# A decode layer's last product in two column groups instead of four, its last weights and a slice of wq cut over other numbers of DMA engines

## The chip, the core and the metric

The kernel runs on one core of one Trainium2 chip. The metric is the device time of one execution in microseconds (us). The core has a matrix engine (PE, with its weight loads PEld), a vector engine (DVE), an activation engine (ACT), a general engine (POOL) and a sequencer that here only issues transfers (SP). Transfers run on 16 DMA engines that all queues share. A transfer that SP issues goes into a queue; each DMA engine that takes part works off its rows in the order of issue and then counts a semaphore up by one.

## What is computed

One decode step (8 batches, one token each) of a layer: attention over the last 2,048 keys of a cache with 32 query heads and 8 key heads, then a feed-forward block. All inputs are bf16. Cut to what is computed:

```python
def A(x, k_cache, v_cache, wq, wo):                  # x: 8 x 1 x 512
    W = 2048
    q = (x @ wq).reshape(8, 1, 32, 128)              # wq: 512 x 4096
    k, v = k_cache[:, :, -W:], v_cache[:, :, -W:]    # 8 x 8 x 2048 x 128 each, heads repeated 4 times
    p = softmax(einsum("bhqd,bhkd->bhqk", q, k) * 128 ** -0.5)
    return einsum("bhqk,bhkd->bhqd", p, v).reshape(8, 1, 4096) @ wo

def B(x, w1, w2, w3, w4):
    # the shifted branch (w1, w2) is zero for one token: x1 = x
    return x + gelu(layernorm(x) @ w3) @ w4          # w3: 512 x 1792, w4: 1792 x 512

h = A_x + A(layernorm(A_x), k_cache, v_cache, wq, wo)
out = h + B(layernorm(h), w1, w2, w3, w4)
```

## The kernel before

The program for each engine is a list written out in the order in which the Python runs; an operation waits for the semaphore values that it names (`Engine.op`, L57, `emit`, L63). There is no scheduler.

**Transfers.** All but x are issued by SP, in one fixed order (L767 to L776): wq, three K tiles, then V and K tiles in turn, three pieces of wo among the last V tiles, w3, and three pieces of w4. A K or V tile is 2 MB, 128 rows of 16 KB; there are 16 of each, in three buffers each, so that a load waits until PE has read what lay in its buffer before. Where nothing else is said a load has 128 rows.

**wq** lies with four of its 512 rows on each of 128 partitions. `load_wq` (L750) brings it in one load without the last `QF` = 1,152 columns of each partition's fourth row; six small loads (the table `FILL`, L44) bring these columns of the 128 rows into `wqF` (L143), a view of the space that w3 will have later. In an entry `(k, h, n)` the source list has `k` outer entries of four rows each, `h` says which 32 partitions and `n` which of `NF` = 3 sections. POOL clears sections 1 and 2 first (L216), and loads with `n` > 0 wait for that.

**Query.** x is normalized and turned (`xlnT`, L263). For the fill the matching columns of x are copied out (`xlnP`, L281), turned by PE (L286) and copied into `xlnF` (L291). PE multiplies wq (L301) in four column groups of 32 output rows that run side by side, then the fill rows (L312) into the second of the two result banks. The result is scaled (L322 ACT, L325 DVE), turned (L335) and laid out (L341, L349).

**Attention.** For each K tile PE turns the keys (L382), ACT and DVE bring them to SBUF (L392, L394), PE makes the scores (L407); softmax runs on DVE and ACT; PE multiplies with V (L503). PE, ACT and DVE do this while the transfers go on.

**End.** After the last V tile come the product with wo (L552), the layer norm (L638 to L682), the product with w3 (L667), gelu (L692, L694) and the product with w4. The residual is added by PE: the sum so far, in two bf16 parts (`fr`, L702 and L703), is multiplied by the identity into the same PSUM space (`pe_fin`, L707). w4 has 14 chunks of 128 rows and comes in pieces of 8, 4 and 2 chunks (`W4_AT`, L715, `load_w4`, L761); the product waits for one semaphore per piece. A chunk is four matmuls of 128 columns, each in a column group of its own (32 PSUM partitions). `pe_fin` stands between the first and the second piece. Then the four results are copied to `out_sb` (L729 to L734), two by DVE and two by ACT, and SP stores them (L779). `warm_end` (L489) puts matmuls without a use between steps; they write to a bank that nobody reads then.

Of the kernel before, what the change touches and what calls it, by code (L numbers as in the profile page):

```python
# [6 lines left out]
dt = mybir.dt  # L7
ACT = mybir.ActivationFunctionType
# [3 lines left out]
B = 8  # L12
D = 512
H = 32
DH = 128
# [7 lines left out]
FC = F // 128  # L23
FG = FC // 2
KC = D // 128
# [14 lines left out]
QW = H - 2 * NQ * R + 1  # L40
QE = QW + NQ * R + NQ * R + QW
AHEAD = NS
QF = 1152
FILL = ((8, 0, 0), (8, 1, 0), (8, 0, 1), (3, 1, 1), (3, 0, 2), (2, 1, 2))  # L44
NF = 3
KF = 64


# [30 lines left out]
def bass_sequential_preLN__sliding_block_cached__mixer_s_mlp__decode_kernel(  # L79
# [23 lines left out]
    with es:  # L103
        sb = lambda shape, dtype, name: es.enter_context(nc.sbuf_tensor(name, shape, dtype))
# [6 lines left out]
        ident_b = sb([128, 128], dt.bfloat16, "ident_b")  # L111
# [9 lines left out]
        w4_sb = sb([128, FC, D], dt.bfloat16, "w4_sb")  # L121
# [17 lines left out]
        rstd = sb([B, 1], dt.float32, "rstd")  # L139

        xlnF = sb([KF, NF, 32], dt.bfloat16, "xlnF")
        xlnP = sb([B, 4 * sum(k for k, _, _ in FILL)], dt.bfloat16, "xlnP")
        wqF = w3_sb[0:KF, 2:4, :].rearrange("p a n -> p (a n)")[:, 0:NF * QF].rearrange("p (s n) -> p s n", s=NF)  # L143
        xlnT = sb([128, KC, 32], dt.bfloat16, "xlnT")
        qrow = sb([128, 2, 512], dt.bfloat16, "qrow")
# [37 lines left out]
        fr = qflat[:, 0:2 * KC * 32].rearrange("p (a n x) -> p a n x", a=2, n=KC)  # L183
        gT = qflat[:, 2 * KC * 32:(2 * KC + FC) * 32].rearrange("p (f x) -> p f x", f=FC)
        out_sb = orow[0:B, 0, :]
# [12 lines left out]
        sem_wf = S("sem_wf")  # L198
# [5 lines left out]
        def dma(eng, dst, src, sem, *waits):  # L204
            def f(e):
                e.dma_start(dst, src).then_inc(sem, 16)  # L206
            eng.op(f, *waits, inc=False)
# [5 lines left out]
        PO.op(lambda e: e.memset(eps2[:], EPS * EPS))  # L213
        e_scr = PO.op(lambda e: e.memset(scratch[:], 1.0))
        e_fz = PO.op(lambda e: e.memset(xlnF[:], 0.0))
        e_wz = PO.op(lambda e: e.memset(wqF[:, 1:NF, :], 0.0))  # L216
        e_xz = PO.op(lambda e: e.memset(xlnT[:], 0.0))
        e_iota = PO.op(lambda e: e.iota(iota_f[:], [[1, 128]], base=0, channel_multiplier=-1,
                                        allow_small_or_imprecise_dtypes=True))
# [50 lines left out]

        def fills():
            at = 0
            for k, h, n in FILL:
                yield k, slice(32 * h, 32 * h + 4 * k), n, at, slice(at, at + 4 * k)
                at += 4 * k

        def q_rows():
            for k, rows, n, at, where in fills():
                a = xln_b[:, :]
                cols = bass.AP(tensor=a.tensor, offset=a.offset + KC * at + KC - 1, ap=[a.ap[0], [KC, k], [KC * k, 4]])  # L280
                e_xP = DV.op(lambda e, cols=cols, where=where: e.tensor_copy(  # L281
                    xlnP[:, where].rearrange("b (e a) -> b e a", a=4), cols))

            def pe_fT(e):
                for k, rows, n, at, where in fills():
                    ins = e.matmul(fT_ps[rows, n * B:(n + 1) * B], xlnP[:, where], ident_b[0:B, 0:B],  # L286
                                   is_transpose=True, tile_position=(0, rows.start))
                return ins
            e = PE.op(pe_fT, e_xP)
            for k, rows, n, at, where in fills():  # L290
                e_fT = DV.op(lambda e, rows=rows, n=n: e.tensor_copy(xlnF[rows, n, 0:B], fT_ps[rows, n * B:(n + 1) * B]),  # L291
                             e, e_fz)
            out = []
            for j in range(2):
                def pe_q(e, j=j):
                    for kc in range(KC):
                        for u in range(4):
                            n = (4 * j + u) * R * DH
                            size = R * DH if kc < KC - 1 else max(0, min(R * DH, H * DH - QF - n))
                            if size:  # L300
                                ins = e.matmul(S_ps[j][32 * u:32 * (u + 1), 0:size], xlnT[:, kc, :], wq_v[:, kc, n:n + size],  # L301
                                               start=(kc == 0), stop=(kc == KC - 1 and size == R * DH),
                                               tile_position=(0, 32 * u), skip_group_check=True)
                    return ins

                def pe_qF(e):
                    for n in range(NF):
                        for u in range(4):
                            w = (u - 4) * R * DH + QF
                            lo = max(0, -w)  # L310
                            if lo < R * DH:
                                ins = e.matmul(S_ps[1][32 * u:32 * (u + 1), lo:R * DH], xlnF[:, n, :],  # L312
                                               wqF[:, n, w + lo:w + R * DH], start=False, stop=(n == NF - 1),
                                               tile_position=(0, 32 * u), skip_group_check=True)
                    return ins
                e_q = PE.op(pe_q, e_xT, (sem_wq, 16))
                if j == 1:
                    e_q = PE.op(pe_qF, e_fT, (sem_wf, 16 * len(FILL)))
                got = S_ps[j][:, :].rearrange("p (r d) -> p r d", r=R)
                for c in range(2):  # L320
                    if j == 0:
                        e = AC.op(lambda e, c=c, got=got: e.activation(qrow2[:, 0, :, c, :], got, ACT.Copy, scale=inv_sqrt_dh),  # L322
                                  e_q)
                    else:
                        e = DV.op(lambda e, c=c, got=got: e.tensor_scalar(qrow2[:, 1, :, c, :], got, inv_sqrt_dh, None,  # L325
                                                                          ALU.mult), e_q)
                out.append(e)
            return out, e_q
# [160 lines left out]
        def warm_end(count):  # L489
            def f(e):  # L490
                for n in range(count):
                    ins = e.matmul(kbank[1], ident_b[:, :], still, start=True, stop=True)  # L492
                return ins
            PE.op(f, e_pT[LAST, 1])
# [178 lines left out]
                      free[2])  # L673
        warm_end(3)
        e_y = [pe_w3(0, FH, e_u, (sem_w3, 16)), pe_w3(FH, FC)]
        warm_end(4)

        e_vs = DV.op(lambda e: e.tensor_reduce(vsum[:, :], vr(st2), AX.X, ALU.add), e_st2)

# [9 lines left out]
        e_gT = []  # L689
# [12 lines left out]
        e_fr = DV.op(lambda e: e.tensor_copy(fr[:, 0, :, 0:B], v3(fin[:, :])), e_fin, e_gz)  # L702
        e_fr = DV.op(lambda e: e.tensor_tensor(fr[:, 1, :, 0:B], v3(fin[:, :]), fr[:, 0, :, 0:B], ALU.subtract), e_fr)  # L703

        z_ps = S_ps[1][:, 0:DH]

        def pe_fin():  # L707
            def f(e):
                for part in range(2):
                    for nb in range(KC):  # L710
                        ins = e.matmul(z_ps[32 * nb:32 * (nb + 1), :], fr[:, part, nb, :], ident_b[:, :],
                                       start=False, stop=False, tile_position=(0, 32 * nb), skip_group_check=True)
                return ins
            PE.op(f, e_fr)
        W4_AT = (0, 8, 12, FC)  # L715
        for n, waits in enumerate(((*e_gT, free[1]), (), ())):
            lo, hi = W4_AT[n:n + 2]
            def pe_w4(e, lo=lo, hi=hi):
                for fc in range(lo, hi):
                    for nb in range(KC):  # L720
                        ins = e.matmul(z_ps[32 * nb:32 * (nb + 1), :], gT[:, fc, :],
                                       w4_sb[:, fc, nb * 128:(nb + 1) * 128], start=(fc == 0), stop=(fc == FC - 1),
                                       tile_position=(0, 32 * nb), skip_group_check=True)
                return ins
            if n == 1:
                pe_fin()
                warm_end(1)
            e_z = PE.op(pe_w4, (sem_w4[n], 16), *waits)
        for nb in range(KC):  # L729
            to, got = out_sb[:, nb * 128:(nb + 1) * 128], z_ps[32 * nb:32 * nb + B, :]  # L730
            if nb % 2:
                e_outa = AC.op(lambda e, to=to, got=got: e.activation(to, got, ACT.Copy), e_z)
            else:
                e_outd = DV.op(lambda e, to=to, got=got: e.tensor_copy(to, got), e_z)  # L734

        def load_k(j):
            dma(SP, knat[:, j % NK, :],
# [12 lines left out]
        def load_wq():  # L750
            size = KC * H * DH - QF
            dma(SP, wbig[:, 0:size], A_wq.rearrange("(p k) n -> p (k n)", k=KC)[:, 0:size], sem_wq)
            for k, rows, n, at, where in fills():
                dma(SP, wqF[rows, n, :],
                    bass.AP(tensor=A_wq.tensor, offset=A_wq.offset + (KC * at + KC - 1) * H * DH + H * DH - QF,
                            ap=[[KC * H * DH, k], [KC * k * H * DH, 4], [1, QF]]), sem_wf, e_wz if n else None)

        def load_w3():
            dma(SP, w3_sb[:, :, :], B_w3.rearrange("(k p) f -> p k f", p=128), sem_w3, e_qturn)
# [1 line left out]
        def load_w4(n):  # L761
            lo, hi = W4_AT[n:n + 2]
            k = W4_RUN[-1] if hi == FC else W4_RUN[0]
            dma(SP, w4_sb[:, lo:hi, :].rearrange("p (g k) n -> p g (k n)", k=k),
                B_w4[lo * 128:hi * 128, :].rearrange("(g p k) n -> p g (k n)", p=128, k=k), sem_w4[n])

        turn = {"K": 0, "V": 0, "O": 0}  # L767
        for kind in "QKKK" + 9 * "VK" + "VKKVKVKVVVOVOO":
# [47 lines left out]
```

## Time and profile before

| | us |
|---|---|
| median of 3 runs (192.88 to 192.95) | 192.91 |
| the profiled execution | 193.01 |
| its span, from the first to the last instruction | 191.6 |
| PE, DVE, ACT, POOL busy | 152.1, 116.4, 95.4, 13.7 |
| wq's bulk: from issue to landing | 11.6 |
| a K tile, a V tile: median from issue to landing | 19.3, 18.8 |
| w4's three pieces: from issue to landing | 32.1, 25.6, 19.2 |
| moved in all | 79.38 MB, 414 GB/s over the span |

The span counts from the first instruction. The time of an execution is longer than its span by what lies around it (1.41 us here). Rows of the timeline give a start, a duration, and, behind "idle before", what ended an engine's wait. A group of instructions has a line of the kernel, an engine, an operation, the tiles written and read with their shapes, a count, and then busy time in us and mean ns of one. Matmuls overlap, so their durations add up to more than the time they take.

### The profile page before, as it was taken

To read this page: it belongs to the slowest core of one execution; us is meant where nothing else is said; L and a number is where in the kernel's file an instruction comes from. 1 tells how busy PE (TensorE), PEld (TensorE's weight loads), DVE (VectorE), ACT (ScalarE), POOL (GpSimd) and SP (SyncE) were. 2 spreads that over 40 slices of the span, in tenths; PEclk is the share of its full clock that TensorE was granted. 3 is DMA by queue.
4 is the path that set the end of the run, shared out by engine and by line. 5 is a ranking of instruction groups with operands and counts; after the bars stand their busy time and mean duration, and the time that the engine had idled before them with its cause. 6 is when DMAs were issued, how large, how long until landed. Compare 5 with 4: busy or idle time off the path is not lost.

```text
span 191.6 us, 3128 instructions
## 1 busy us (share of the span) xinstructions
PE 152.1 (79%) x1302; PEld 93.0 (49%) x1302; DVE 116.4 (61%) x259; ACT 95.4 (50%) x124; POOL 13.7 (7%) x37
## 2 busy tenths in 40 slices
PE   0049999698978878688878887989899895697995
PEld 0013966366546445454555454645555562233262
DVE  2733354843788358745985586557865886756333
ACT  3002567648365726492559254754692676430251
POOL 8400200100010001000100010002000000000040
PEclk9999999969999999999999997899999999999999
DMA  6989999999999999999999999999999999999991
GB/s 243 452 377 434 434 428 434 431 429 414 434 438 431 431 428 431 422 431 428 438 434 424 431 428 434 424 428 438 426 424 434 434 431 426 426 431 421 410 407 71
DMA packets 6477, 79.38 MB, mean 414 GB/s; under 512 B 688, under 2 KB 704, under 8 KB 1856
## 3 DMA queue, kind: packets, MB, share of 16 engines
q1 hardware_dynamic: 6448, 79.18, 97.3%
q8 instruction: 10, 0.16, 0.3%
q14 instruction: 3, 0.02, 0.0%
q10 hardware_dynamic: 16, 0.01, 0.0%
HBM read 79.18 MB, written 0.01 MB: 413 GB/s over the span
## 4 chain that ended last, share of the span: by engine, by line
DMA 49%; PE 23%; DVE 11%; SPq 9%; ACT 6%; issue 1%
DMA knat<-in_A_k_cache_dram 33%; PE kT_ps L382 10%; DMA w_sb<-in_B_w_dram 10%; SPq L206 9%; DMA wbig<-in_A_wq_dram 6%; ACT pT_sb L471 4%; DVE kT_sb L394 3%; PE o_rows L503 3%; PE S_ps L503 3%; ACT kT_sb L392 2%; PE S_ps L407 2%; PE S_ps L301 2%; DVE oacc L515 2%; DVE mblk L430 1%; DVE omask L513 1%
## 5 line engine op out<-in xcount | busy, mean ns | idle before, releaser
L392 ACT ACTIVATE kT_sb<-kT_ps 128x1024 bf16<-128x1024 bf16 x64 | 65.7, 1027 | 55.2 <-PE kT_ps L382 55.1
L382 PE MATMUL kT_ps<-turn_f,knat 128*128 128x128 f32 x512 | 76.0, 289 | 14.8 <-DMA knat<-in_A_k_cache_dram 9.7
L382 PEld LDWEIGHTS kT_ps<-turn_f,knat 128*128 128x128 f32 x512 | 59.0, 146 | 35.3 <-DMA knat<-in_A_k_cache_dram 13.1
L394 DVE COPY kT_sb<-kT_ps 128x1024 bf16<-128x1024 bf16 x64 | 43.8, 685 | 24.6 <-PE kT_ps L382 24.3
L407 PE MATMUL S_ps<-kT_sb,qblk 128*32 128x512 bf16 x256 | 25.9, 398 | 0.5 <-DVE kT_sb L394 0.5
L503 PE MATMUL o_rows<-vnat,pT_sb 128*64 128x512 bf16 x128 | 15.4, 381 | 6.1 <-ACT pT_sb L471 6.1
L471 ACT ACTIVATE pT_sb<-o_rows,own_f 128x512 bf16<-128x512 f32 x28 | 17.7, 697 | 1.3 <-PE o_rows L466 1.2
L515 DVE TENSOR_REDUCE oacc<-omask 128x128 f32<-128x512 f32 x14 | 14.9, 1061 | 0.5
L503 PEld LDWEIGHTS o_rows<-vnat,pT_sb 128*64 128x64 bf16 x128 | 8.1, 110 | 12.0 <-issue 8.4
L349 POOL COPY qblk<-qT 64x64 bf16<-64x64 bf16 x16 | 5.0, 311 | 119.9 <-PE S_ps L407 107.0
L503 PE MATMUL S_ps<-vnat,pT_sb 128*64 128x512 bf16 x112 | 13.4, 382 | 0.0
L513 DVE TENSOR_TENSOR omask<-o_rows,own_s 128x512 f32<-128x512 f32 x7 | 4.8, 686 | 13.1 <-PE o_rows L503 13.1
L407 PEld LDWEIGHTS S_ps<-kT_sb,qblk 128*32 128x32 bf16 x256 | 6.5, 93 | 11.5 <-issue 7.2
L513 DVE TENSOR_TENSOR omask<-S_ps,own_s 128x512 f32<-128x512 f32 x7 | 4.8, 692 | 7.9 <-PE S_ps L503 7.9
L503 PEld LDWEIGHTS S_ps<-vnat,pT_sb 128*64 128x64 bf16 x112 | 5.8, 110 | 6.2 <-issue 1.6
L439 ACT ACTIVATE E_sb<-S_ps,negM 128x512 f32<-128x512 f32 x8 | 5.5, 690 | 6.4 <-DVE negM L435 6.4
L322 ACT ACTIVATE w_sb<-S_ps 128x512 bf16<-128x512 f32 x2 | 1.1, 594 | 11.5 <-PE S_ps L301 11.5
L258 PE MATMUL sm<-ident_b,xln_b 8*128 8x8 bf16 x4 | 0.3, 174 | 8.0 <-DVE xln_b L233 8.0
L528 PE MATMUL sm<-oacc,sel_o 128*128 128x256 f32 x16 | 6.1, 466 | 0.6 <-DVE oX L535 0.6
L492 PE MATMUL kT_ps<-ident_f,ident_b 128*128 128x512 bf16 x24 | 6.5, 380 | 0.0
L558 ACT ACTIVATE orow<-kT_ps 128x512 bf16<-128x512 f32 x1 | 0.6, 597 | 11.3 <-PE kT_ps L552 11.3
L430 DVE TENSOR_REDUCE mblk<-S_ps 128x1 f32<-128x512 f32 x8 | 5.4, 681 | 0.8 <-PE S_ps L407 0.8
(117 smaller groups left out, 103.3 us busy)
## 6 DMA issues: line engine op xcount, KB each, us to landing
knat<-in_A_k_cache_dram SPq DMA_DIRECT2D x16, 2048.0 KB, 19.3
vnat<-in_A_v_cache_dram SPq DMA_DIRECT2D x15, 2048.0 KB, 18.8
wbig<-in_A_wq_dram SPq DMA_DIRECT2D x1, 3808.0 KB, 11.6
wbig<-in_A_wo_dram SPq DMA_DIRECT2D x2, 1024.0 KB, 22.5
knat<-in_A_v_cache_dram SPq DMA_DIRECT2D x1, 2048.0 KB, 19.8
wbig<-in_A_wo_dram SPq DMA_DIRECT2D x1, 2048.0 KB, 24.0
w_sb<-in_B_w_dram SPq DMA_DIRECT2D x1, 1792.0 KB, 30.1
w_sb<-in_B_w_dram SPq DMA_DIRECT2D x1, 1024.0 KB, 32.1
```

The lines of the kernel that those rows point to most:

```text
L206: e.dma_start(dst, src).then_inc(sem, 16)
L382: ins = e.matmul(kT_ps[i % 2][:, n * 256:(n + 1) * 256].bitcast(dt.float32), knat[:, j % NK, c * DH:(c + 2) * DH].bitcast(dt.float32), tur ...
L392: e_lo[i] = AC.op(lambda e: e.activation(kT_sb[:, i % NKT, 0:W // 2], kT_ps[i % 2][:, 0:W // 2], ACT.Copy), e_Tlo[i], e_QK.get(i - NKT))
L394: e_hi[i] = DV.op(lambda e: e.tensor_copy(kT_sb[:, i % NKT, W // 2:W], kT_ps[i % 2][:, W // 2:W]), e_Thi[i], e_QK.get(i - NKT))
L407: ins = e.matmul(S_ps[b % 2][32 * t:32 * (t + 1), :], qblk[:, b % 2, KQ * q + t, half, at:at + H], kT[:, :, t, :, half], start=(q == 0 and ...
L430: e = DV.op(lambda e: e.tensor_reduce(mblk[:, 0:1], S_ps[b % 2][:, :], AX.X, ALU.max), e_QK[G * b + G - 1], e_mz)
L471: e_pT[b, t] = AC.op(lambda e: e.activation(pT_sb[:, b % 2, :, H * t:H * (t + 1)], bank[:, :].rearrange("p (n y) -> p n y", n=NN), ACT.Cop ...
L492: ins = e.matmul(kbank[1], ident_b[:, :], still, start=True, stop=True)
L503: ins = e.matmul(bank[64 * u:64 * (u + 1), :], pT_sb[:, b % 2, n, :].rearrange("p (x q) -> p q x", q=NQ)[:, q, :], v_tile(m)[:, n * 512:(n ...
L513: free[at] = DV.op(lambda e: e.tensor_tensor(omask[:, :, :], bank.rearrange("p (s d) -> p s d", s=NS), own, ALU.mult), e_PV[m], e_acc.get( ...
L515: e_acc[m] = DV.op(lambda e: e.tensor_reduce(acc, omask[:, :, :].rearrange("p s d -> p d s"), AX.X, ALU.add), free[at], e_O.get(b - 2))
L528: e_O[b] = PE.op(lambda e: e.matmul(O_ps, sel_o[:, :], oacc[:, b % 2, :, :].rearrange("p q d -> p (q d)"), start=True, stop=True), e_acc[N ...
```

## The change

Four edits:

- **The last product** has two column groups of 256 columns (PSUM partitions 0 to 31 and 64 to 95) in place of four of 128. A chunk is two matmuls; the residual's eight matmuls write into the same two groups. The first piece's product is cut at chunk 7, where the second half of gelu begins, so that the first seven chunks wait for the first half alone. Two copies of 256 columns, one on DVE and one on ACT, take the place of four of 128.
- **w4's last piece** (two chunks, 128 rows of 2 KB) is loaded as 104 rows and 24 rows, both on the semaphore of that piece.
- **wq**: the bulk load leaves out 512 columns of every fourth row (`QF`) in place of 1,152. Three loads bring these: the entries `(k, h, n, ns)` have `k` outer entries and `ns` sections, 60, 60 and 8 rows of 1 KB, with 3, 3 and 2 outer entries. There are six sections; POOL clears all of them, and all three loads wait for that. The copies around it go section by section or for all sections of an entry at once.
- **Spin products**: three in place of four between w3 and w4, and the one behind `pe_fin` is gone.

```diff
-QF = 1152
-FILL = ((8, 0, 0), (8, 1, 0), (8, 0, 1), (3, 1, 1), (3, 0, 2), (2, 1, 2))
-NF = 3
+QF = 512
+FILL = ((3, 0, 0, 5), (3, 1, 0, 5), (2, 0, 5, 1))
+NF = 6
+LAST_W4 = (0, 104, 128)
...
-        e_wz = PO.op(lambda e: e.memset(wqF[:, 1:NF, :], 0.0))
+        e_wz = PO.op(lambda e: e.memset(wqF[:, :, :], 0.0))
...
-                e_xP = DV.op(lambda e, cols=cols, where=where: e.tensor_copy(
-                    xlnP[:, where].rearrange("b (e a) -> b e a", a=4), cols))
+                e_xP = DV.op(lambda e, cols=cols, at=at, k=k, ns=ns: e.tensor_copy(
+                    xlnP[:, at:at + 4 * k * ns].rearrange("b (n e a) -> b n e a", n=ns, a=4), cols))
 
             def pe_fT(e):
-                for k, rows, n, at, where in fills():
-                    ins = e.matmul(fT_ps[rows, n * B:(n + 1) * B], xlnP[:, where], ident_b[0:B, 0:B],
-                                   is_transpose=True, tile_position=(0, rows.start))
+                for k, rows, n0, ns, at in fills():
+                    for n in range(ns):
+                        ins = e.matmul(fT_ps[rows, (n0 + n) * B:(n0 + n + 1) * B],
+                                       xlnP[:, at + 4 * k * n:at + 4 * k * (n + 1)], ident_b[0:B, 0:B],
+                                       is_transpose=True, tile_position=(0, rows.start))
...
-        warm_end(4)
+        warm_end(3)
...
-        z_ps = S_ps[1][:, 0:DH]
+        z_ps = S_ps[1][:, 0:D // 2]
...
-                        ins = e.matmul(z_ps[32 * nb:32 * (nb + 1), :], fr[:, part, nb, :], ident_b[:, :],
-                                       start=False, stop=False, tile_position=(0, 32 * nb), skip_group_check=True)
+                        u, h = divmod(nb, 2)
+                        ins = e.matmul(z_ps[64 * u:64 * u + 32, h * 128:(h + 1) * 128], fr[:, part, nb, :],
+                                       ident_b[:, :], start=False, stop=False,
+                                       tile_position=(0, 64 * u), skip_group_check=True)
...
-        for n, waits in enumerate(((*e_gT, free[1]), (), ())):
-            lo, hi = W4_AT[n:n + 2]
+        PARTS = ((0, FH, 0, (e_gT[0], free[1])), (FH, 8, 0, (e_gT[1],)), (8, 12, 1, ()), (12, FC, 2, ()))
+        for lo, hi, n, waits in PARTS:
             def pe_w4(e, lo=lo, hi=hi):
                 for fc in range(lo, hi):
-                    for nb in range(KC):
-                        ins = e.matmul(z_ps[32 * nb:32 * (nb + 1), :], gT[:, fc, :],
-                                       w4_sb[:, fc, nb * 128:(nb + 1) * 128], start=(fc == 0), stop=(fc == FC - 1),
-                                       tile_position=(0, 32 * nb), skip_group_check=True)
+                    for u in range(2):
+                        ins = e.matmul(z_ps[64 * u:64 * u + 32, :], gT[:, fc, :],
+                                       w4_sb[:, fc, u * (D // 2):(u + 1) * (D // 2)],
+                                       start=(fc == 0), stop=(fc == FC - 1),
+                                       tile_position=(0, 64 * u), skip_group_check=True)
                 return ins
             if n == 1:
                 pe_fin()
-                warm_end(1)
-            e_z = PE.op(pe_w4, (sem_w4[n], 16), *waits)
-        for nb in range(KC):
-            to, got = out_sb[:, nb * 128:(nb + 1) * 128], z_ps[32 * nb:32 * nb + B, :]
-            if nb % 2:
-                e_outa = AC.op(lambda e, to=to, got=got: e.activation(to, got, ACT.Copy), e_z)
-            else:
-                e_outd = DV.op(lambda e, to=to, got=got: e.tensor_copy(to, got), e_z)
+            e_z = PE.op(pe_w4, (sem_w4[n], 16 * (len(LAST_W4) - 1) if hi == FC else 16), *waits)
+        e_outd = DV.op(lambda e: e.tensor_copy(out_sb[:, 0:D // 2], z_ps[0:B, :]), e_z)
+        e_outa = AC.op(lambda e: e.activation(out_sb[:, D // 2:D], z_ps[64:64 + B, :], ACT.Copy), e_z)
...
-            for k, rows, n, at, where in fills():
-                dma(SP, wqF[rows, n, :],
+            for k, rows, n, ns, at in fills():
+                dma(SP, wqF[rows, n:n + ns, :],
                     bass.AP(tensor=A_wq.tensor, offset=A_wq.offset + (KC * at + KC - 1) * H * DH + H * DH - QF,
-                            ap=[[KC * H * DH, k], [KC * k * H * DH, 4], [1, QF]]), sem_wf, e_wz if n else None)
+                            ap=[[KC * H * DH, k], [KC * k * H * DH, 4 * ns], [1, QF]]), sem_wf, e_wz)
...
-            dma(SP, w4_sb[:, lo:hi, :].rearrange("p (g k) n -> p g (k n)", k=k),
-                B_w4[lo * 128:hi * 128, :].rearrange("(g p k) n -> p g (k n)", p=128, k=k), sem_w4[n])
+            for p0, p1 in zip(LAST_W4, LAST_W4[1:]) if hi == FC else ((0, 128),):
+                dma(SP, w4_sb[p0:p1, lo:hi, :].rearrange("p (g k) n -> p g (k n)", k=k),
+                    B_w4[lo * 128:hi * 128, :].rearrange("(g p k) n -> p g (k n)", p=128, k=k)[p0:p1], sem_w4[n])
```

## The prediction

> **What bounds the kernel now.** I read the page first. The DMA row is full in every slice but the first two and the last.
>
> ```profile
> span 191.6 us, 3128 instructions
> PE 152.1 (79%) x1302; PEld 93.0 (49%) x1302; DVE 116.4 (61%) x259; ACT 95.4 (50%) x124; POOL 13.7 (7%) x37
> DMA  6989999999999999999999999999999999999991
> DMA packets 6477, 79.38 MB, mean 414 GB/s; under 512 B 688, under 2 KB 704, under 8 KB 1856
> ...
> q8 instruction: 10, 0.16, 0.3%
> ```
>
> No compute engine is above 79%; the 16 DMA engines are. The end, from the chain of waits:
>
> ```profile
> 169.96 19.22 DMA w_sb<-in_B_w_dram
> 189.18 0.04 issue
> 189.22 0.32 PE S_ps L721 x8
> 189.54 0.02 issue
> 189.57 0.28 DVE orow L734
> 189.84 0.03 issue
> 189.88 0.28 DVE orow L734
> ```
>
> The last piece of w4 lands at 189.18; eight matmuls, two copies and the store follow. The view by windows shows the 16 engines not ending together (columns: window, length, busy us of five engines, clock, DMA share, GB/s):
>
> ```profile
> 185.00:186.00 1.00, 1.00 (x32) 1.00 (x33) 0.10 (x1) 1.00 (x1) 1.00 (x1) 1.00 0.99 406
> 186.00:187.00 1.00, 1.00 (x31) 0.88 (x30) 0.29 (x2) 0.42 (x2) 0.63 (x1) 1.00 0.86 344
> 187.00:188.00 1.00, 1.00 (x26) 0.46 (x27) 0.81 (x5) 0.25 (x1) 0.00 (x0) 1.00 0.50 197
> 188.00:189.00 1.00, 1.00 (x49) 0.60 (x37) 0.00 (x0) 0.00 (x0) 0.00 (x0) 1.00 0.22 78
> ```
>
> So the end is that of the most loaded engine, and what counts is how many bytes each engine carries. The trace's packet records and semaphore updates tell it. Packets of one engine follow each other without a gap: 16,384 B every 0.607 us, 30,464 B 1.124, 4,096 B 0.155, 2,304 B 0.090, 2,048 B 0.080; the next DMA begins 0.006 us behind the completion packet of the one before. A DMA is split in equal shares of whole rows. wq's six extra loads give 38 updates, six from issuing and 8+8+8+3+3+2 from engines (the page's 688 packets under 512 B are the completions: 40 DMAs of 16, these 32, and 8 each for x and the store). They nest: the first K tile lands on eight engines at 16.80 to 17.14, on five at 17.78 to 17.99, on one at 18.44, on two at 19.05 and 19.10. So the fills lie on the lowest engines: 0 and 1 have 24 rows of 2,304 B, engine 2 has 20, 3 to 7 have 12, 8 to 15 none.
>
> From there each engine keeps its phase tile after tile, except that each of PE's instruction loads (q8, 16 KB) sets one engine back by 1.42 us. Followed tile by tile, eight engines are hit in turn: two of the upper eight, two of 3 to 7, four of the upper eight, then (the load at 180.50) the first of them again. That engine, hit twice, lands at 189.18. Next come 188.91 and 188.89 (one of 0 and 1, and one of 3 to 7, both also hit by smaller instruction loads). The trace does not name which of 8 to 15 the last engine is; the change treats these eight in three ways, so the forecast hangs on that.
>
> **The change, part by part.** The profiled execution took 193.01 (span 191.6 and 1.41 around it); the median of the runs shown is 192.91, 0.10 lower. I add my differences to both.
>
> *wq.* The bulk row grows from 30,464 to 31,744 B. Slope between two rows: (1.124 - 0.607)/14,080 B, so 0.047 a row, eight rows on each engine: +0.375 for all. The fills: 1,024 B rows are not in any load of wq before; from 2,048 B (0.080) and the slope I take 0.042 (the 1,024 B rows of x and of the store last 0.044 to 0.101, where rows did not queue; lower end 0.037 by bandwidth alone, upper 0.060). Engines 0 and 1 get 20+20+4 rows: 1.85 instead of 24 x 0.090 = 2.16; with completions -0.33. Engine 2: 40 rows, -0.12. Engines 3 to 7: 12 x 0.090 and 3 completions gone, -1.10. Upper eight: nothing to lose.
>
> *w4's last piece.* 128 rows on 16 engines were 8 x 0.080 + 0.006 = 0.646 each. Equal shares of 104 rows over at most 16 engines are 13 engines of 8 rows; 24 rows are 12 of 2. If they start from engine 0 as the fills do, 0 to 11 get +0.166, 12 stays, 13 to 15 lose 0.646.
>
> [...]
>
> Together, in us at the end of each engine's queue: 0 and 1: +0.21; 2: +0.42; 3 to 7: -0.56; 8 to 11: **+0.54**; 12: **+0.375**; 13 to 15: **-0.27**.
>
> *Last product.* Its groups, before:
>
> ```profile
> L721 PE MATMUL S_ps<-w_sb,qrow 128*32 128x128 bf16 x56 | 1.3, 221 | 0.1
> L503 PE MATMUL o_rows<-vnat,pT_sb 128*64 128x512 bf16 x128 | 15.4, 381 | 6.1 <-ACT pT_sb L471 6.1
> L734 DVE CAST orow<-S_ps 8x128 bf16<-8x128 f32 x2 | 0.6, 282 | 1.7 <-PE S_ps L721 1.7
> L732 ACT ACTIVATE orow<-S_ps 8x128 bf16<-8x128 f32 x2 | 0.5, 270 | 2.2 <-PE S_ps L721 2.1
> L325 DVE TENSOR_SCALAR w_sb<-S_ps 128x512 bf16<-128x512 f32 x2 | 1.3, 686 | 5.5 <-PE S_ps L312 5.5
> L216 POOL MEMSET w_sb<- 64x2304 bf16 x1 | 2.0, 2015 | 0.0
> ```
>
> Four matmuls of 128 columns run side by side, one set every 0.056 us in the trace; sixteen of 512 in two groups (L503) take 1.94, 0.22 a pair. A pair of 256 columns is then 0.11 by step and 0.27 by duration (0.219 and 128 columns more at the 0.42 ns of the step). The last piece has two steps: 0.295 becomes 0.38, **+0.09** (upper end +0.30 if two groups that are not neighbours do not overlap; lower 0). The copies: 0.60 for two on DVE. 128 columns cost 0.282, 512 cost about 0.65 to 0.69 (L325), so 256 cost 0.40, ACT likewise 0.38: **-0.20** (ends -0.10 to -0.30: a copy of 256 is dearer than one of 128 and cheaper than two). Tail: -0.11.
>
> Ahead of it PE needs 8 x 0.11 = 0.88 where it took 0.45 for the first eight chunks, and 0.22 for the residual product. The landing of w4's first piece moves with the bulk, 187.34 to 187.72; PE is done at 187.76 + 1.10 = 188.86, just before the second piece (188.59 + 0.375 = 188.96). So it is covered by that wait, with 0.1 to spare. The two spin products fewer fill time in which PE waits.
>
> *Start.* L216 grows by a third, 2.02 to 2.69, and now all fills wait for it: three issues of 0.79 from 3.63 end at 6.0, where six ended at 5.92; behind them in SP's queue K's first load is issued at 6.0 instead of 5.96, and the engines are busy with wq until 11.4. On POOL iota and on DVE the chain to xlnT come 0.7 later (10.0 to 10.7), six small copies fewer give back about 0.7, and wq lands at 12.7. The six 512-column fill products go into one column group, one behind the other: L301 shows a set of 512 columns every 0.43 us this early, so 2.6 where nine took 1.46. With the bulk PE is some 1.6 late at the first K tile. What waits for that is SP, with K's fourth load (issued at 24.93); the first engine needs it at 31.07. Six us of queued transfers cover it, and from 36.5 PE waits for K again. Were that cover gone, 1.6 would be lost. SP's extra issue near 174 has 14 us of queue before it. I cost all this at nothing.
>
> **Forecast.** Four of the eight possible engines are 8 to 11: the last one then lands 0.54 later at 189.72, tail -0.11: +0.43, 193.44 against the profiled execution, **193.34** on the runs. Terms' ends give 193.15 to 193.6.
>
> **Rivals.**
> - *The last engine is 12.* It loses no row: +0.375 - 0.11 = +0.27, 193.18. If the turn of the hits climbs, the fifth of six upper engines is 12 to 14; if it falls, 9 to 11. The trace does not say which.
> - *The other side: the last engine is one of 13 to 15, relieved of w4's last rows.* It is then done with everything at 188.61, and engines 0 and 1 set the last landing, 188.59 + 0.21 + 0.30 = 189.10. But its second piece still lands at 188.96, four chunks of it follow, and PE runs all six steps from 189.0: 5 x 0.11 + 0.27 = 189.83 against 189.51, copies -0.20: +0.1, 193.03, no change that can be measured. It decides as soon as that engine has no rows of the last piece; the 0.646 freed is the price.
> - *The instruction load at 180.50 moves.* PE has three matmuls more by then and thus is earlier in its program; if it struck another engine, or none that is late, 0 and 1 would set the end and PE would not: -0.08 - 0.11, 192.72. Against: three of some 1,250 matmuls shift it by well under a us.
> - *Small rows cost more.* At 0.080 a row of 1,024 B, 44 rows are +1.7 on engines 0 and 1: 194.4. The 2,048 B rows at 0.080 speak against it.
> - *The second DMA of w4's last piece pays a latency of its own.* The trace has 0.006 between queued DMAs, so nothing; 0.3 is the lag from completion packet to update, paid once either way. If it were paid again: 193.6.
>
> [...]
>
> **How the numbers follow.** Chances: 8 to 11, 0.45; 12, 0.18; 13 to 15, 0.20; load moved, 0.07; small rows or an own latency or a lost start, 0.10. A measurement of this kernel tells about 0.2% (0.39 us) from no change, so slower begins at 193.30: most of the first case and nearly all of the last, with a little of 12, 0.48. Faster ends at 192.52, below all terms, 0.07 for what I overlook. The rest, 0.45, is within. The range 192.7 to 193.7 holds the first four cases and part of the last; the likeliest alone is 193.15 to 193.6.
>
> **What would show it.** Updates of the last piece: 13 and 12 from engines. Its last landing at 189.7 (8 to 11), 189.55 (12) or 189.1 (13 to 15), and whether PE waits for it or still works on the piece before. One copy of 0.40 on DVE and one of 0.38 on ACT. A first K tile that lands on engines 3 to 7 together with the upper eight; fills of 0.042 a row. DMA slices full from 12 to 185; a gap near 31 would show that the late start is not covered. I am wrong if the engine that lands last is not the one hit twice.

## The result and the profile after

| | before | after |
|---|---|---|
| median of 7 runs each, us | 192.88 (192.74 to 192.95) | 193.74 (193.69 to 194.79) |
| ratio of the times, 95% interval | 1 | 1.0056 (1.0041 to 1.0070) |
| the profiled execution | 193.01 | 193.69 |
| its span | 191.6 | 192.4 |

The change costs 0.86 us by the medians and 0.68 by the two profiled executions, which is more than the 0.2% that can be told here. Single executions over 1 us longer occur with most of the kernels below, the kernel before among them (3 of 29 near 194.3 in one session), so medians are given.

The page of the kernel after first. The shares of the engines hardly move, and the DMA row is full as before:

```profile
span 192.4 us, 3057 instructions
PE 151.8 (79%) x1268; PEld 93.8 (49%) x1275; DVE 115.6 (60%) x252; ACT 95.3 (50%) x123; POOL 14.5 (8%) x37
DMA  6999999999999999999999999999999999999991
```

The end of its chain of waits (start, length, what):

```profile
162.65 26.96 DMA w_sb<-in_B_w_dram
189.65 0.85 PE S_ps L727 x12
```

The DMA that releases the last matmuls is another one than before. Then it was the last piece of w4, issued at 169.96, with eight matmuls behind it; now it is the second piece, issued at 162.65, with the twelve matmuls of both pieces behind it. The semaphore updates say the same: the second piece's last one comes at 189.60 (before: 188.59), the last piece's at 189.50 (before: 189.18). In the kernel before all 16 engines end w4's pieces in the order of issue (their updates, paired in order of time, lie 1.23 to 1.29 and then 0.59 to 0.65 apart). By that order the engine that ends the second piece at 189.60, after the last update of the last piece, had no row of the last piece. That piece counted 13 and 12 updates from engines, as forecast.

The windows near the end (window, length, five engines' busy us, clock, DMA share, GB/s) hold what was not foreseen:

```profile
185.00:186.00 1.00, 0.78 (x23) 0.78 (x24) 0.07 (x1) 1.00 (x1) 1.00 (x1) 1.00 1.00 408
186.00:187.00 1.00, 1.00 (x37) 1.00 (x35) 0.22 (x1) 0.39 (x2) 0.60 (x1) 1.00 0.85 295
187.00:188.00 1.00, 0.85 (x11) 0.23 (x7) 0.69 (x4) 0.25 (x1) 0.00 (x0) 1.00 0.70 238
188.00:189.00 1.00, 0.73 (x14) 0.68 (x16) 0.19 (x1) 0.00 (x0) 0.00 (x0) 1.00 0.26 92
```

From 186 to 187 the engines are as busy as before (0.85 against 0.86) but move 295 GB/s, not 344: packets take longer. The packet records show where. Before, all 384 packets of 4,096 B (w4's first two pieces) lasted about 0.159 and all 128 of 2,048 B 0.084. After, 63 of the 384 last up to 0.332 and 54 of the 128 up to 0.154, all begun between 186.04 and 188.46, while some engines already work on the last piece (its packets begin from 185.53 on) and others still on the pieces before it (theirs begin until 188.93). (Durations of packets; their steps are the 0.155 and 0.080 of the prediction.)

The timeline of the tail (start, duration, engine, what; in brackets what ended the wait):

```profile
188.27 1.05 PE L727 MATMUL S_ps<-w_sb,qrow 128*32 128x256 bf16 x16 [0.42 <-DMA w_sb<-in_B_w_dram]
189.15 0.39 PE L716 MATMUL S_ps<-ident_b,qrow 128*32 128x128 bf16 x8
189.65 0.83 PE L727 MATMUL S_ps<-w_sb,qrow 128*32 128x256 bf16 x12
190.52 0.38 ACT L736 ACTIVATE orow<-S_ps 8x256 bf16<-8x256 f32 x1 [2.81 <-PE S_ps L727]
190.52 0.41 DVE L735 CAST orow<-S_ps 8x256 bf16<-8x256 f32 x1 [2.32 <-PE S_ps L727]
191.03 0.29 SPq L782 DMA_DIRECT2D out_dram<-orow  x1
```

PE waits 0.42 for the first piece (its last landing 188.23, before 187.34), then for the second, and has six chunks, of two matmuls each, left. The copies take 0.41 and 0.38 where two on DVE took 0.60.

At the start, two groups answer to the prediction's (busy us, mean ns of one, idle before):

```profile
L316 PE MATMUL S_ps<-w_sb,xlnF 64*32 64x512 bf16 x6 | 2.7, 627 | 0.0
L217 POOL MEMSET w_sb<- 64x3072 bf16 x1 | 2.7, 2657 | 0.0
```

The clearing took 2.66, the fills were issued from 3.70, K's first load at 6.20, and PE came to the first K tile at 21.4 (1.8 later than before). K's fourth load went out at 27.37 instead of 24.93, and the engines moved 433 GB/s from 26 to 31 and 419 from 31 to 36 (before: 436 and 429), with busy shares of 1.02 and 0.98: the cover held.

### The profile page after: what moved, and what is told of

The parts are those of the page before. It is cut to its first block, busy times and chain, and to the rows that moved or that the text cites. A ratio compares the mean times of both kernels' runs of the same rounds, so it can differ in the third digit from the quotient of the medians.

```text
span 192.4 us, 3057 instructions
## 1 busy us (share of the span) xinstructions
PE 151.8 (79%) x1268; PEld 93.8 (49%) x1275; DVE 115.6 (60%) x252; ACT 95.3 (50%) x123; POOL 14.5 (8%) x37
## 4 chain that ended last, share of the span: by engine, by line
DMA 61%; PE 20%; DVE 7%; SPq 5%; ACT 4%; issue 1%
DMA knat<-in_A_k_cache_dram 31%; DMA w_sb<-in_B_w_dram 14%; DMA vnat<-in_A_v_cache_dram 10%; PE kT_ps L386 9%; DMA wbig<-in_A_wq_dram 6%; SPq L207 5%; ACT pT_sb L475 2%; ACT kT_sb L396 2%; PE o_rows L507 2%; PE S_ps L411 2%; PE S_ps L507 2%; DVE kT_sb L398 2%; PE S_ps L305 2%; PE S_ps L316 1%; DVE oacc L519 1%; DVE mblk L434 1%
## 5 line engine op out<-in xcount | busy, mean ns | idle before, releaser
L496 PE MATMUL kT_ps<-ident_f,ident_b 128*128 128x512 bf16 x22 | 5.9, 379 | 0.0
```

## The experiments

"Before" is the kernel before on the same chip in the same session.

### Which of the edits costs

**The change without the split of w4's last piece.**

```diff
-LAST_W4 = (0, 104, 128)
+LAST_W4 = (0, 128)
```

> The changed kernel with w4's last piece again in one load of 128 rows; all else as changed. Theory (the split slows packets: a load of 104 rows spreads its rows over the engines in another way than a load of 128, so that two engines write to one place): every 4,096 B and 2,048 B packet of w4 lasts 0.159 and 0.084 again; the engine hit twice has the last piece again and lands last, at 189.18 + 0.375 = 189.56; PE's tail costs 0.09 more and the copies 0.20 less than before; 192.9 + 0.27 = 193.15. Rival (another part of the change slows them, such as the fills of wq, or PE's new reading of w4): the slow packets stay and the time stays at 193.6 or above.

193.27 (12 runs, 193.01 to 194.54), 0.12 above what was expected; before 192.88; ratio 1.0030 (1.0011 to 1.0049). Not one packet of w4 is slow. The second piece lands at 188.87, the last at 189.45. The theory's reason, two engines that write to one place, is the author's guess; no run shows it. So by the medians 0.47 of the 0.86 is the split's (193.74 - 193.27), and the second piece lands 0.73 earlier without it. From 186 to 187 the engines move 336 GB/s with a busy share of 0.82, against 295 with 0.85 in the change:

```profile
186.00:187.00 1.00, 1.00 (x35) 1.00 (x34) 0.22 (x1) 0.99 (x2) 1.00 (x1) 1.00 0.82 336
```

**The split alone, in the kernel before** (the same edit of `load_w4` and its semaphore count).

> The kernel before with nothing but w4's last piece as 104 and 24 rows. Theory: slow packets, the second piece lands 0.3 to 0.7 late (188.9 to 189.3) and PE works both pieces off behind it: 193.0 to 193.3. Rival (the split itself is harmless and relieves the last engine): the last landing comes to 189.06, 192.8.

193.37 (12 runs), a little above what was expected; before 192.88; ratio 1.0018 (1.0008 to 1.0028). Slow packets again (4,096 B up to 0.373), second piece at 189.08 instead of 188.59, last at 189.61 instead of 189.18. From 187 to 188 the engines move 184 GB/s with a busy share of 0.54, where the kernel before moves 197 with 0.50:

```profile
187.00:188.00 1.00, 1.00 (x35) 0.54 (x37) 0.67 (x5) 0.25 (x1) 0.00 (x0) 1.00 0.54 184
```

By the medians the split costs about as much without any of the other edits, 0.49.

**The change with 96 and 32 rows**, which 16 engines can share equally, 6 and 2 rows each.

```diff
-LAST_W4 = (0, 104, 128)
+LAST_W4 = (0, 96, 128)
```

> The changed kernel with w4's last piece as 96 and 32 rows, which 16 engines can share evenly (6 and 2 rows each), so that each engine carries as many bytes as with one load of 128. Theory (what matters is which rows an engine gets): packets of w4 slow down again, 0.2 to 0.3 us for 4,096 B, and the time is above that with one load, 193.3 to 193.8. Rival (the uneven load on 13 engines is what slows): no slow packet, 193.15 as with one load.

194.59 (6 runs, 193.77 to 195.51), above what was expected; ratio 1.0081 (1.0052 to 1.0109). By these shares no engine is relieved and none gets more, yet the slow packets are there (4,096 B up to 0.341) and the second and the last piece land at 190.09 and 190.60. So the slow packets do not come from the unevenness of the shares. Not all of this time need be the DMA's: in the profiled execution the granted clock was 0.50 from 187 to 190, and the first sixteen matmuls of w4's product took 1.69 instead of 1.05.

**The wq edit alone, in the kernel before.**

> The kernel before with nothing but the change to wq (bulk without 512 columns in place of 1,152, three loads of 1 KB rows on 3, 3 and 2 engines). Theory (my sum for the engines): every engine's bulk takes 0.375 more, the engine hit twice (one of 13 to 15) has no fill rows to lose, so its last landing moves from 189.18 to 189.56; the four-group tail is as before: 192.88 + 0.375 = 193.25. The late start of PE (1.7 us at the first K tile) stays covered: no gap in the transfers near 31. Rival (the late start is not covered, or 1 KB rows slow engines 0 and 1): 193.6 to 194.6, with packets of 1,024 B well over 0.042 or an engine that waits between two tiles.

193.29 (12 runs), before 192.96; ratio 1.0019 (1.0003 to 1.0036): +0.33 of the forecast 0.375. Last landing 189.41 (+0.23), no slow packets of w4. The fills are loads of 60, 60 and 8 rows on 3, 3 and 2 engines (in the change, which has the same fills, their semaphore counts eight updates from engines beside three from issuing); all their 128 packets of 1,024 B last 0.046, and the packets of the K tiles that move beside them last 0.611. So not every load of fewer than 128 rows slows packets; these few ran on two or three engines each.

**The tail alone, in the kernel before** (two groups, two copies, the spins as in the change). It was run twice.

> The kernel before with nothing but the last product in two groups of 256 columns, its two copies and the fewer spin products. Theory (my sum of the tail): last matmul 0.09 later behind the last landing, copies 0.20 shorter: -0.11, 192.8. Rival (PE becomes the bound in the last product, since its chunks cost 0.11 in place of 0.056): PE still works on the second piece when the last lands, 193.0 to 193.2.

> The kernel before with the last product in two groups alone, once more for an undisturbed profile. My sum of the tail: from last landing to last matmul 0.38 + 0.04 in place of 0.33, copies 0.41 in place of 0.60: -0.1. If PE is the bound it starts on the last piece later than 0.04 behind its landing, and the time is 192.9 or more.

192.97 against 192.88, ratio 1.0000 (0.9989 to 1.0011), and 192.84 against 192.96, ratio 0.9993 (0.9973 to 1.0014): no change that can be told. The timeline of the second run shows why the cheaper copies bring nothing:

```profile
187.72 1.05 PE L723 MATMUL S_ps<-w_sb,qrow 128*32 128x256 bf16 x16
188.60 0.39 PE L712 MATMUL S_ps<-ident_b,qrow 128*32 128x128 bf16 x8
188.83 0.82 PE L723 MATMUL S_ps<-w_sb,qrow 128*32 128x256 bf16 x12
```

No bracket stands behind these rows: PE works from 187.72 to 189.65 without a wait. It takes up the second piece at 188.83, which had landed at 188.52, and it ends 0.54 behind the landing of the last piece (189.11). The kernel before begins this product at the same time, with shorter matmuls:

```profile
187.71 0.63 PE L721 MATMUL S_ps<-w_sb,qrow 128*32 128x128 bf16 x32
```

There the first eight chunks take 0.45 and PE then waits for both later pieces; with two groups they take 0.88, and no wait is left in which the cheaper copies could show. What stands ahead of the product is the spin matmuls, 186.98 to 187.79, while w4's first piece landed at 187.27. Three of them end when four do in the kernel before, because w3's product began later, at 185.19 instead of 184.93 (w3 landed at 184.77). The windows show one possible reason (clock third from the end):

```profile
164.00:168.00 4.00, 4.00 (x18) 1.50 (x18) 2.59 (x7) 0.45 (x2) 0.00 (x0) 0.50 1.04 440
```

At half its clock PE is busy all the time here. The runs of the wq edit alone and of the split alone, with the old tail, have 0.61 and 0.67 in the same window, so this need not come from the tail's edit.

By the medians the parts add up: 0.33 for wq, 0 for the tail, 0.49 for the split make 0.82 of the 0.86. By the ratios they make 0.7 of 1.1, which their intervals allow, so the shares are good to some tenths of a microsecond.

### What the split disturbs

**A V tile as two loads of 64 rows**, in the kernel before, to enlarge the effect. (Not shown, here and in the next three runs: what waits for this tile's buffer counts 16 more.)

```diff
             if m == 6:
-                dma(SP, v_tile(m), src, V(m)[0], e_PV.get(m - NV))
+                dma(SP, v_tile(m)[0:64, :], src[0:16], V(m)[0], e_PV.get(m - NV))
+                dma(SP, v_tile(m)[64:128, :], src[16:32], V(m)[0])
```

> The kernel before with one V tile (the seventh) as two loads of 64 rows in place of one of 128. Each of the 16 engines then has 4 rows of each load, 8 in all, as before. [...] Rival (the slow packets of w4 came from where they are read in HBM, or from small rows of 2 and 4 KB alone): 0.611 throughout, 192.9.

200.11 (2 runs), ratio 1.0364 (1.0324 to 1.0404): +7.2, more than packets of twice their 0.611 would give by estimate (eight on each engine, 4.9). The windows:

```profile
82.00:86.00 4.00, 3.26 (x32) 2.09 (x32) 1.38 (x2) 3.57 (x6) 0.00 (x0) 1.00 1.07 377
86.00:90.00 4.00, 0.72 (x8) 0.17 (x3) 1.71 (x2) 0.00 (x0) 0.00 (x0) 1.00 1.00 217
90.00:94.00 4.00, 3.27 (x20) 1.76 (x22) 0.69 (x1) 1.02 (x1) 0.00 (x0) 0.67 1.02 221
```

All 16 engines are busy, and they move 217 GB/s, half of the 428 to 434 of the windows before. Packets of 16,384 B that last 0.611 elsewhere last up to 1.299 from 84 to 99, 15 us, in which 217 GB/s are 3.3 MB: more than the 2 MB of this tile, so the loads beside it are slowed as well.

**The same tile as two loads of 128 rows with half of the columns each.**

```diff
-                dma(SP, v_tile(m)[0:64, :], src[0:16], V(m)[0], e_PV.get(m - NV))
-                dma(SP, v_tile(m)[64:128, :], src[16:32], V(m)[0])
+                dma(SP, v_tile(m)[:, 0:4096], src[:, :, 0:4096], V(m)[0], e_PV.get(m - NV))
+                dma(SP, v_tile(m)[:, 4096:8192], src[:, :, 4096:8192], V(m)[0])
```

> The kernel before, with the same V tile as in the run of two 64-row loads cut the other way: two loads of all 128 rows, each with half of a row's columns (8,192 B pieces). Theory (a load of fewer than 128 rows gives its rows to engines in another way, and these engines then collide): with 128 rows nothing collides; 8,192 B packets at about 0.31 us each ((16,384 B at 0.607) halved, 0.304 and a little), 16,384 B packets stay at 0.61, every stretch from 70 to 100 us at 400 GB/s or more, time 192.9 to 193.1. Rival (two loads of a tile cost by themselves, by their number or by their halved pieces): slowed packets again and a time near 200. Rival (half-length pieces are dearer): 256 of them above 0.33, so at least 16 x 0.03 = +0.5 on each engine, 193.4.

193.03 (10 runs), before 192.98; ratio 0.9995 (0.9976 to 1.0014). The same window:

```profile
86.00:90.00 4.00, 3.53 (x36) 2.19 (x34) 1.93 (x3) 2.22 (x3) 0.00 (x0) 1.00 1.00 424
```

Two loads in place of one cost nothing here; the two loads of 64 rows did.

**Two loads of 64 rows with the first writing to the even partitions, the second to the odd ones**, and **two loads of 64 rows that write as in the first of these runs but read every other group of four rows.** In both, rows of this one tile change places.

```diff
+                dma(SP, v_tile(m)[0:128:2, :], src[0:16], V(m)[0], e_PV.get(m - NV))
+                dma(SP, v_tile(m)[1:128:2, :], src[16:32], V(m)[0])
```

```diff
+                dma(SP, v_tile(m)[0:64, :], src[0:32:2], V(m)[0], e_PV.get(m - NV))
+                dma(SP, v_tile(m)[64:128, :], src[1:32:2], V(m)[0])
```

> The V tile of the slow run again as two 64-row loads, and each load reads the same rows of the cache as there, but the first writes to the even partitions and the second to the odd ones (so the rows of this tile change places, and the attention over them is another). If the collision is at the partitions that are written: 64 rows now reach all 128 partitions in steps of two, 16,384 B packets stay near 0.61 us, 192.9 to 194. If it is at the addresses that are read, or lies in the number of rows: packets up to 1.3 us again, stretches near 217 GB/s, 200.

> The same tile as two 64-row loads that write to partitions 0 to 63 and 64 to 127 as in the slow run, but the first reads every other group of four rows of the cache and the second the groups between (rows of this tile change places). Partitions written: slow as before, 199 to 201, stretches near 217 GB/s. Addresses read: 192.9 to 194. Number of rows alone: slow in this run and in the one before.

200.27 and 200.33 (one execution each), before 192.92. From 86 to 90 they moved 209 and 217 GB/s, with packets of up to 2.04 and 1.31. Reading every other group does not help, so it is not that a load reads groups that lie side by side in the cache. Writing to all 128 partitions in steps of two does not help either. What the three runs near 200 us share is 64 rows over 16 busy engines (share 0.99 to 1.00 from 86 to 90), by equal shares four rows of each load on every engine.

### Can the tail's part be had?

**The kernel before with the tail, and no spins between w3's and w4's product.**

```diff
-        warm_end(4)
```

> The kernel before with the product in two groups and the two copies, and the spin products between w3's and w4's product and within w4's product left out, so that PE comes to w4's first product earlier. Theory (in the run with the tail alone PE worked through without a pause from w4's first product to the end, so the cheaper copies could not show): PE waits for w4's last piece again, its last 8 matmuls start within 0.1 of the last landing at 189.1 to 189.2, end 0.38 later, copies 0.4: end 0.1 to 0.15 earlier than before, 192.75 to 192.85. Rival (PE is still behind, because the compute chain from the last V tile, not the spins, sets its start): last landing before PE's last 8 matmuls by over 0.1, and 192.85 to 193.0. Rival (fewer spins let the granted clock fall): products of w4 at 1.5 to 2 times their duration, over 193.1.

193.72 (12 runs), before 192.98; ratio 1.0018 (0.9995 to 1.0042). The runs fall in two groups: four from 192.61 to 193.03, eight from 193.56 to 194.15. The profiled one (193.97) is of the second. Its windows and the last product's rows:

```profile
187.00:188.00 1.00, 0.67 (x8) 0.49 (x10) 0.76 (x5) 0.25 (x1) 0.00 (x0) 0.52 0.56 215
188.00:189.00 1.00, 1.00 (x12) 0.70 (x10) 0.00 (x0) 0.00 (x0) 0.00 (x0) 0.50 0.13 51
...
187.33 1.89 PE L721 MATMUL S_ps<-w_sb,qrow 128*32 128x256 bf16 x16 [0.49 <-DMA w_sb<-in_B_w_dram]
189.44 1.31 PE L721 MATMUL S_ps<-w_sb,qrow 128*32 128x256 bf16 x12
```

PE starts 0.39 earlier than with the spins, and then at half its clock: 1.31 for the twelve matmuls that took 0.82. So the second rival held in this execution. The clock fell at 187.03, in the pause of 0.49 that the spins had filled. The four short ones have a mean of 192.77, 0.2 below the median of the kernel before; which clock they had over the last product is not recorded.

**That kernel with w4's last piece as two loads of 128 rows and one chunk each.**

```diff
-        W4_AT = (0, 8, 12, FC)
+        W4_AT = (0, 8, 12, 13, FC)
...
+            if lo >= 12:
+                dma(SP, w4_sb[:, lo, :], B_w4[12 * 128:FC * 128, :].rearrange("(p k) n -> p k n", k=2)[:, lo - 12, :], sem_w4[n])
```

> The run before this one, with w4's last piece as two loads of 128 rows and one chunk (1,024 B pieces) each, instead of one load of two chunks. Theory (it is the 104 and 24 rows that collide, not that the last piece is two loads): every packet of w4 at its usual duration (4,096 B 0.159), 1,024 B ones at 0.046, 16 x 0.042 + 2 x 0.006 instead of 8 x 0.080 + 0.006 on each engine: last landing 0.04 later; against that PE has one chunk fewer behind it, so 192.7 to 192.9, the same as the run before it within 0.1. Rival (a second load for the last piece has a price of its own): slowed packets of 4,096 B, second piece at 189.0 or later, 193.2 or more.

193.45 (12 runs, 192.61 to 194.07), above what was expected, ratio 1.0016 (0.9997 to 1.0036); the profiled execution has the low clock again, from 188.12 on. All 384 packets of 4,096 B last 0.159 and all 256 of 1,024 B 0.046; the last landing is 189.12, as in the run before it. A second load for the last piece has no price in these; 104 and 24 rows have.

**Both again with two spin matmuls** where the kernel before had four.

```diff
-        warm_end(4)
+        warm_end(2)
```

> The kernel before with the product in two groups and the two copies, two spin matmuls of 512 columns between w3's and w4's product where before had four, and none within w4's product. [...] Rival (the compute chain sets the start of w4's product, not the spins): start at 187.6 or later, no pause before the last matmuls, 192.85 to 193.0. Rival (clock halves as without spins): 12 matmuls in 1.3 instead of 0.82, 193.5 to 194.

> The run before this one with w4's last piece as two loads of all 128 rows and one chunk (1,024 B) each. All packets at their usual durations; last landing 0.04 later, four matmuls instead of eight behind it (0.11 fewer): 0.05 to 0.1 below the run before it, 192.6 to 192.8. If TensorE is late anyway: the same as the run before it or 0.05 more.

192.84 (12 runs, eleven of them 192.68 to 192.95) and 192.82 (ten of 12 from 192.62 to 192.91), before 192.92; ratios 0.9996 (0.9980 to 1.0011) and 0.9997 (0.9986 to 1.0007). The difference is 0.08 and 0.10, in the direction of a gain and below what can be told. Both profiled executions (194.06, 194.15) had the clock at 0.50 from 188 to 190 (0.50 and 0.59 from 187 to 188), so for the usual ones the start of the product is not known. No pause like the 0.49 without spins stands before it: in the first, PE was busy for 3.34 of the 3.44 us before the clock fell at 186.94. No version here is shown to beat the kernel before.

## Why the prediction failed where it did

- **The bound** (the most loaded DMA engine's queue sets the end): right. The chain after ends in a DMA of w4 and the last matmuls behind it.
- **wq, +0.375 on every engine**: right in kind, somewhat too large. Alone it cost 0.33 by the medians and 0.23 at the last landing. The fill rows were sized right (0.046 as packets, one every 0.042), and the first K tile lands on 13 engines together (16.95 to 17.66), then on one at 18.93 and two at 19.08 and 19.34: engines 3 to 7 with the upper eight, as said.
- **Start at nothing**: right; PE was 1.8 late instead of 1.6, with no gap near 31.
- **Which engine is last**: the likeliest case, 8 to 11, was wrong; it is one of 13 to 15 by the prediction's numbers (the rival at 0.20), since the last engine has no rows of w4's last piece. The numbers are labels: the landings show which loads share engines, and no trace names one, so which of the three it is stays open. The instruction load at 180.51 again hit an engine that had been hit before.
- **w4's last piece**: the step that failed. The sum took rows times 0.080, 0.166 more for some engines and 0.646 less for others, and let packets last as before: the second piece "still lands at 188.96". It landed at 189.60. The premise that a packet's duration does not depend on which rows the other engines move was never named as a premise, and no rival stood for it. The runs show the price: without the split the second piece lands at 188.87 and no packet is slow; with it alone, in the kernel before, 59 of w4's 512 packets are slow and 0.49 is lost. A relief of 0.646 was bought for three engines, and one of them gained nothing from it, because w4's second piece was slowed on the way.
- **Last product and copies**: the durations were right (0.88 for eight chunks, 0.83 for six, copies 0.41 and 0.38). As a gain of 0.11 it did not show: "covered by that wait, with 0.1 to spare" did not hold without the split. With the tail alone PE reached the second piece at 188.83, 0.31 behind its landing; in the change without the split it reached it at 189.10, 0.23 behind. PE then set the end. In the change itself PE does wait, so there the tail is as forecast: 1.33 from the second piece's landing to the end of the copies (189.60 to 190.93), where the rival's sum gives about 1.3.

The right rival with the right landing gives the result: 191.6, +0.1 as that rival said, +0.64 for the late second piece, 192.34; the span is 192.4. The likeliest case, 193.34 and at most 193.6, was short by 0.40, and the range ended 0.04 below the median. That it came this close is luck: it had another engine last, for another reason.

What the runs leave open is why loads of 104, 96 or 64 rows slow the engines down. Excluded as the only cause are two loads in place of one, uneven shares, the reading of neighbouring groups, and that half of the partitions alone is reached. Fewer rows than 128 are not enough either, as wq's fills show. That what 64 rows show is also what 104 and 24 rows do rests on the same kind of slow packets, not on a run that links them.

## What to carry to other kernels

When a load of 128 rows has to be cut, cut it by columns or by chunks: no packet slowed down in the two runs that did so (424 GB/s at a share of 1.00; 0.159 and 0.046 a packet), while cuts by rows cost 0.5 us on 256 KB and 7 us on 2 MB. But wq's fills are loads of few rows too, and no packet slowed down there (0.046), so look at the packets in each case. When an edit gives some DMA engines less to do, ask not only for the bytes of each but whether the packets around it keep their duration, and read it as GB/s beside the busy share in the same window. A gain behind the last landing is worth something only while PE waits for that landing (the tail alone: 192.97 against 192.88, 192.84 against 192.96); look whether the row of the last matmuls has a wait at all.

## What the runs showed of the hardware that was not expected

- Two loads of 64 rows halve what 16 busy DMA engines move (217 instead of 428 to 434 GB/s), and the engines' busy share stays at 1.00.
- wq's fills, loads of 60, 60 and 8 rows on 3, 3 and 2 engines, slow nothing: 0.046 for each of their packets, 0.611 for those of the K tiles beside them.
- The stretches of 0.50 in the granted clock, in executions that have 1.00 elsewhere, last 3.41 us or twice that where they end before the kernel does. In five profiled executions with the two-group tail (three, two and no spins between w3's and w4's product) the clock fell between 186.86 and 188.12, each time 20.48 us after the end of the stretch of 0.50 before it, which ended between 166.38 and 167.64. In two with the old tail and its four spins that stretch ended at 166.66 and 167.09, and the clock did not fall; in the others it ended at other times. Without spins 8 of 12 executions took 193.56 to 194.15 and the others 193.03 or less; with two spins 1 and 2 of 12 were above 193.5. What decides is not shown.
